# P times V of a sliding-window attention, from whole 128-key tiles to two row tiles of 64 keys, in a gated mixer kernel on one core

## The chip, the cores and the metric

The kernel runs on one NeuronCore of a Trainium2 chip. TensorE (PE, with its weight loads shown as PEld), VectorE (DVE), ScalarE (ACT), GpSimd (POOL) and the DMA queues that SyncE (SP) and ACT start work side by side and wait for one another through semaphores. The metric is the device time of one execution in microseconds (us), lower is better; a time is given as the median of several runs.

## The reference

An attention branch A (2048 tokens, 512 channels, 32 heads of 16 channels, a causal window of 256 keys), an MLP branch B (LayerNorm, 512 to 1792, GELU, back to 512), and a gate between them, all in float32:

```python
qkv = (x @ wqkv).reshape(B, S, 3, H, Dh)          # H = 32, Dh = 16, S = 2048
scores = einsum("bhqd,bhkd->bhqk", q, k) * Dh ** -0.5
mask = (idx[:, None] - idx[None, :] >= 0) & (idx[:, None] - idx[None, :] < 256)
p = softmax(where(mask, scores, -1e9))
a = einsum("bhqk,bhkd->bhqd", p, v).reshape(B, S, D) @ wo
h = gelu(layernorm(x) @ w1 + b1)                  # F = 1792
b = h @ w2 + b2
g = sigmoid((x * gate_w).sum(-1))
out = g * a + (1 - g) * b
```

A key reaches the 256 queries from its own on. So a tile of 128 keys reaches 128 + 256 = 384 queries, and a tile of 64 keys 64 + 256 = 320.

## The kernel before, in words

The work falls into three stages.

**First stage.** The projections to q, k and v (`qk_unit` line 302, `v_unit` line 334), the row statistics, and the splits of the inputs. Most products are made from float32 values split into a high and a low part (type fp32r), three matmuls for one; P times V is not split, both of its operands are plain float32. The values V stand in one tile `vs` of 16 blocks of 128 keys, with 17 columns to a head: 16 channels and a column of ones (`memset`, line 583), so that the same product also gives the row sums of P.

**Second stage.** It works off four kinds of steps, in an order that is written out by hand in the string `ORDER` (`run`, line 748):

- `S` (`s_pair`, line 353): scores of one block of 128 queries for two heads, only to find the largest score of each query: two matmuls in row tiles of 64 partitions side by side (line 362), then a masked copy and a maximum on DVE (lines 371 and 372). Every fourth block of queries its maxima go through DRAM into the operands of the next kind of step (`put_max`).
- `T` (`st_pair`, line 409): the transposed scores, 128 keys by up to 384 queries for two heads (line 418), exp on ACT (line 420) into a tile of P (eight slots, `p_tile`), and POOL sets what lies outside the window to zero (line 422). Two `T` steps fill one P tile of a block of keys kb and a group p of four heads.
- `P` (`pv`, line 429): P times V of a group p of four heads for the 256 queries with number j, or for 512 queries where two `P` stand side by side in the string and j is even. The four heads of a group are four column tiles of 32 columns. For 256 queries four blocks of keys count, one *step* each: 256, 128, 256 and 128 queries wide; for 512 queries six steps. At j = 0 the two steps before the first query fall away. A step is four matmuls, one for each head, and the trace shows each of these float32 matmuls as two weight loads and two matmuls. The product stands in the first bank of a pair of banks, is copied out on ACT (line 136, through `copy`), in the last steps on DVE (line 451), and is put beside its neighbour in one of two staging buffers (`sums`, names x in the profile), so that 512 queries are stored by one DMA of 256 KB into `osc` in DRAM (line 458, or 460 at the end).
- `f` (`fill`, line 719): one of the 24 steps of an MLP unit (`mlp1_unit`, line 639): two matmuls in row tiles of 64 partitions, 512 wide (line 651). The result goes through ACT to `hp` in DRAM.

PSUM is four pairs of banks. `S`, `T` and `P` each take the next pair of a ring (`two`, line 117; the string `PICK` says where the second in the ring is taken in place of the first); an MLP unit holds one pair for its 24 steps. A pair comes free when its reader (ACT or DVE) is done.

**Last stage.** 56 items (c, f): a chunk c of 512 tokens and a block f of 128 hidden channels. For each, `hp` is loaded (`load_h`, six items ahead), GELU runs on ACT (line 707), DVE splits it (lines 711 and 133), and PE does 12 matmuls of 512 columns (`mlp2`, line 881). The second weights come by `load_w2`, six items ahead, for the first chunk only. All of these take their buffers from one ring of 28 tiles `t`. Beside this, once for each chunk, `attn_out` (line 817) loads the row sums `su` and the products `oa` from `osc`, DVE takes the reciprocal (line 833), it goes through DRAM to `ra`, DVE multiplies (line 839), ACT and DVE split the result, and PE multiplies by wo (line 850), 12 matmuls for each of the four blocks of 128 tokens. At the end of a chunk line 889 (first chunk) or 895 takes the sum out of PSUM.

## Time and profile before

| | us |
|---|---|
| median of 3 runs (lowest, highest) | 690.24 (689.75, 690.57) |
| the profiled execution | 689.64 |
| its span, first to last instruction | 687.8 |
| first stage, until the first P times V comes near | 0 to 149 |
| second stage | 149 to 484 |
| last stage | 484 to 687.8 |

The granted TensorE clock was 0.999 of full speed over the span. What lies around the span is 1.84 us. How to read the rows that follow in the prediction: in a table of stages each engine has its busy time and, in brackets, its number of instructions; then come the granted clock, the mean busy share of the DMA engines and GB/s. A row of the time line starts with the start of a group of instructions and the time from its first start to its last end, so groups that overlap in the pipelined PE have times that overlap. A matmul's record runs on after its last column has entered, so the pace of PE is read from one start to the next and not from lengths. `128x256 f32 x8` means eight matmuls 256 columns wide with 128 partitions of contraction, `64*128 64x512` one with 64 partitions.

### The profile page before, as it was taken

The numbers are of one execution on the slowest core, as the hardware profiler recorded it, in microseconds if no ns is written. First come the engines' busy times: TensorE is split into PE (matmuls) and PEld (weight loads), VectorE is DVE, ScalarE is ACT, GpSimd is POOL, SyncE is SP. The second block draws the span as 40 slices with busy tenths as digits, with TensorE's granted clock in tenths as the row PEclk, the third lists the DMA queues.
The fourth block names the chain that finished last, engine by engine and source line by source line (L and its number), as shares of the span: only waits on it lengthen the run. The fifth ranks groups of instructions, "written<-read, shape, count | busy, mean of one in ns | idle before, by whom it ended". The sixth has DMA issues, their size and how long they took to land.

```text
span 687.8 us, 15593 instructions
## 1 busy us (share of the span) xinstructions
PE 681.1 (99%) x5674; PEld 535.5 (78%) x5674; DVE 476.4 (69%) x970; ACT 384.6 (56%) x637; POOL 265.9 (39%) x622
## 2 busy tenths in 40 slices
PE   9999999999999999999999999999999999999997
PEld 6887777877768777877787777777787888888886
DVE  6737789968777787777686877855575545556454
ACT  6438453457677776877758777687633224123231
POOL 6800156426666664765656566568000000000000
PEclk9999999999999999999999999999999999999999
DMA  8998888786575767566676555527876450841801
GB/s 322 354 290 266 278 262 267 217 253 224 176 211 173 247 211 228 174 214 188 190 240 207 168 185 153 178 96 240 288 238 204 143 173 5 275 126 41 253 1 62
DMA packets 89620, 137.91 MB, mean 200 GB/s; under 512 B 13160, under 2 KB 36648, under 8 KB 89416
## 3 DMA queue, kind: packets, MB, share of 16 engines
q1 hardware_dynamic: 81384, 128.72, 59.1%
q10 hardware_dynamic: 8160, 8.19, 3.9%
q8 instruction: 45, 0.74, 0.4%
q14 instruction: 31, 0.25, 0.1%
HBM read 81.53 MB, written 54.30 MB: 197 GB/s over the span
## 4 chain that ended last, share of the span: by engine, by line
PE 96%; ACT 1%; DVE 1%; DMA 1%; issue 0%; POOL 0%; SPq 0%; DVEq 0%; ACTq 0%
PE ps_b L651 22%; PE ps_a L881 22%; PE ps_b L441 13%; PE ps_d L308 12%; PE ps_b L418 7%; PE ps_b L362 7%; PE ps_d L338 7%; PE ps_o L850 6%; PE ps_d L295 1%; PE ps_x L362 1%; DMA qk<-qk 1%; PE ps_x L279 1%; ACT x L420 0%; DVE us L895 0%; DVE us L889 0%; ACT pb L420 0%
## 5 line engine op out<-in xcount | busy, mean ns | idle before, releaser
L651 PE MATMUL ps_b<-x,w 64*128 64x512 f32 x1344 | 207.1, 393 | 0.0
L881 PE MATMUL ps_a<-x,t 128*128 128x512 f32 x648 | 150.2, 389 | 0.2 <-DVE t L711 0.2
L372 DVE TENSOR_REDUCE mx<-ps_b 128x2 f32<-128x512 f32 x208 | 144.1, 693 | 7.1
L881 PEld LDWEIGHTS ps_a<-x,t 128*128 128x128 f32 x648 | 121.5, 188 | 26.2 <-DVE t L711 0.6
L651 PEld LDWEIGHTS ps_b<-x,w 64*128 64x128 f32 x1344 | 127.4, 186 | 10.5 <-ACT x L136 0.3
L371 DVE COPY_PREDICATED ps_b<-tri,ps_b 128x256 f32<-128x256 uint8 x208 | 88.4, 425 | 52.7 <-PE ps_b L362 40.6
L422 POOL TENSOR_SCALAR_AFFINE_SELECT pa<-pa 128x256 f32<-128x256 f32 x192 | 74.2, 414 | 57.7 <-ACT pa L420 56.7
L420 ACT ACTIVATE pa<-ps_b 128x768 f32<-128x768 f32 x96 | 76.5, 813 | 24.7 <-PE ps_b L418 13.3
L418 PE MATMUL ps_b<-qk 50*128 50x384 f32 (+5 forms) x512 | 87.8, 339 | 0.1
L308 PE MATMUL ps_d<-x,w 128*128 128x512 f32 x360 | 84.7, 390 | 0.0
L362 PE MATMUL ps_b<-qk 62*128 62x384 f32 (+3 forms) x472 | 83.0, 345 | 1.0 <-DMA qk<-qk 0.8
L308 PEld LDWEIGHTS ps_d<-x,w 128*128 128x128 f32 x360 | 67.3, 188 | 14.5 <-issue 0.5
L420 ACT ACTIVATE pb<-ps_b 128x768 f32<-128x768 f32 (+2 forms) x96 | 66.2, 706 | 20.5 <-PE ps_b L418 9.7
L422 POOL TENSOR_SCALAR_AFFINE_SELECT pb<-pb 128x256 f32<-128x256 f32 x160 | 62.2, 415 | 37.4 <-ACT pb L420 36.9
L707 ACT ACTIVATE t<-t,b1s 128x512 f32<-128x512 f32 x56 | 38.6, 716 | 44.0 <-DMA t<-hp 43.6
L418 PEld LDWEIGHTS ps_b<-qk 50*128 50x128 f32 (+1 forms) x512 | 48.8, 184 | 16.0 <-issue 3.2
L422 POOL TENSOR_SCALAR_AFFINE_SELECT x<-x 128x256 f32<-128x256 f32 x128 | 49.3, 414 | 29.7 <-ACT x L420 29.3
L420 ACT ACTIVATE x<-ps_b 128x768 f32<-128x768 f32 x64 | 50.7, 813 | 14.0 <-PE ps_b L418 9.7
L362 PEld LDWEIGHTS ps_b<-qk 62*128 62x128 f32 (+1 forms) x472 | 45.1, 184 | 17.2 <-issue 3.9
L338 PE MATMUL ps_d<-wv,x 128*128 128x512 f32 x192 | 46.7, 394 | 0.0
L850 PE MATMUL ps_o<-w,t 128*128 128x512 f32 x192 | 46.1, 389 | 0.0
L441 PE MATMUL ps_b<-pa,v 128*32 128x128 f32 (+2 forms) x704 | 42.9, 345 | 0.3 <-ACT x L420 0.2
(96 smaller groups left out, 757.1 us busy)
## 6 DMA issues: line engine op xcount, KB each, us to landing
qk<-qk SPq DMA_DIRECT2D x112, 196.0 KB
t<-hp SPq DMA_DIRECT2D x56, 256.0 KB
hp<-t SPq DMA_DIRECT2D x54, 256.0 KB
qk<-t SPq DMA_DIRECT2D x48, 256.0 KB
osc<-x SPq DMA_DIRECT2D x31, 256.0 KB
t<-in_w SPq DMA_DIRECT2D x28, 256.0 KB
w<-w SPq DMA_DIRECT2D x28, 256.0 KB
qk<-t ACTq DMA_DIRECT2D x24, 256.0 KB
```

The lines of the kernel that those rows point to most:

```text
L308: pe.matmul(o, a[:, dt * 128:(dt + 1) * 128], b[:, dt * C:(dt + 1) * C], start=n == 0, stop=n == 11)
L338: pe.matmul(o, x[:, a:a + 128], wvs[dt][:, k], start=n == 0, stop=n == 11)
L362: pe.matmul(o[:, e, :n], qs[pr][r:k, qb * 128:qb * 128 + 128], ks[pr][r:k, t0:t0 + n], start=True, stop=True)
L371: dve.copy_predicated(o[:, :, :128], tri, o[:, :, 256:384])
L372: dve.tensor_reduce(m, o[:, :, :256], mybir.AxisListType.X, ALU.max)
L418: pe.matmul(o[:, e, :w], ks[pr][r:k, kb * 128:kb * 128 + 128], qs[pr][r:k, kb * 128:kb * 128 + w], start=True, stop=True)
L420: act.activation(pt[:, :, :w], o[:, :, :w], AF.Exp, scale=0.25)
L422: pool.affine_select(out=pt[:, :, a:a + 128], in_=pt[:, :, a:a + 128], pattern=[[0, 2], [sgn, 128]], base=b, channel_multiplier=-sgn, comp ...
L441: pe.matmul(a[32 * h:32 * h + 32, at:at + w], vs[:, kb, v:v + 32], pts[p, kb][:, h, fr:fr + w], start=n == 0, stop=n == len(parts) - 1, sk ...
L651: pe.matmul(o[:, e], w[kt // 4][r:r + 64, k, m:m + 128], y[r:r + 64, a:a + C], start=n == 0, stop=n == 23)
L850: pe.matmul(a, x[:, g], wos[g][:, k], start=n == 0, stop=n == 11)
L881: pe.matmul(accs[c][b], x[:, b * 128:(b + 1) * 128], w, start=f == 0 and n == 0, stop=f == FT - 1 and n == 2)
```

## The change

P times V is now cut into two row tiles of 64 keys. The upper and the lower 64 keys of a block each take only the 320 queries that they reach, in two row tiles of the array (rows 0 to 63 and 64 to 127), with the four heads still in four column tiles: eight matmuls in a step in place of four, each with half of the contraction. The upper half of the keys adds into the first bank of the pair, the lower half into the second, and the steps are sorted so that pieces of the same or nearly the same width stand together: for 256 queries 256, 192, 128 and 64 wide. Nothing on the chip adds the two banks in this stage: both are copied (one ACT copy of 2 x 256 columns for each 256 queries) and stored as halves, one DMA of 256 KB for each 256 queries. `osc` is laid out anew and twice as large. There are still two staging buffers, but each now holds 256 queries; where a third copy comes up with two stores still unissued, the oldest store is issued first. The copy on DVE in the last steps is gone, all copies are on ACT.

In the last stage both halves are loaded (eight DMAs of 256 KB for the products of a chunk, four for the sums, two writes of the reciprocals) and DVE adds them: one add of 128x128 before the reciprocal and one of 128x512 ahead of each multiplication of line 839. To make room the ring of 28 tiles becomes rings of their own: 8 for the loads of `hp`, 6 for the split parts, 5 for the raw second weights and 4 for the rest; the second weights are loaded four items ahead in place of six.

`ORDER` and `PICK` are new. Both orders have 652 `f`, 256 `T`, 236 `S` and 63 `P` letters, and one `P` more runs after each.

The rows below show one P times V as PE has it, the same one (heads 0 to 3, queries 768 to 1023) before and now, with the steps around it; pa, pb and x are slots of P tiles, v is V, ps_b a pair of banks, qk the score operands. Before:

```order
L362 MATMUL ps_b_262_1541<-qk_79 128x384 x2
L418 MATMUL ps_b_261_1535<-qk_79 128x384 x2
L441 MATMUL ps_b_260_1529<-x_254_1522,v_80 32x256 x4
L441 MATMUL ps_b_260_1529<-pb_1524,v_80 32x128 x4
L441 MATMUL ps_b_260_1529<-pb_1524,v_80 32x256 x4
L441 MATMUL ps_b_260_1529<-pb_1524,v_80 32x128 x4
L362 MATMUL ps_b_263_1546<-qk_79 128x384 x2
```

The same place in the changed kernel, where line 418 has become 420, 362 has become 364 and 441 has become 450:

```order
L364 MATMUL ps_b_260_1530<-qk_79 128x384 x2
L450 MATMUL ps_b_261_1536<-pb_1524,v_80 32x256 x4
L450 MATMUL ps_b_261_1536<-x_254_1522,v_80 32x256 x4
L450 MATMUL ps_b_261_1536<-x_254_1522,v_80 32x192 x4
L450 MATMUL ps_b_261_1536<-pb_1524,v_80 32x192 x4
L450 MATMUL ps_b_261_1536<-pb_1524,v_80 32x128 x8
L450 MATMUL ps_b_261_1536<-pb_1524,v_80 32x64 x8
L364 MATMUL ps_b_262_1541<-qk_79 128x384 x2
```

There are 16 matmuls before and 32 now; each pair of rows (or an x8) is one step of two row tiles, and the widths of a step's row tile come to 640 in place of 768.

The next rows are ACT's at the place in the second stage where the copies of P times V stand closest together. L136 (L138 now) is the copy of a bank, with x_253 and x_254 the staging buffers where a ps_b is copied to x; the copies to t are those of an MLP unit, and L420 (L422 now) is the exp. Before:

```order
L136 ACTIVATE t_1811<-ps_b_263_1546 128x512
L136 ACTIVATE t_1814<-ps_b_263_1546 128x512
L420 ACTIVATE pb_1524<-ps_b_261_1535 128x768
L136 ACTIVATE x_253_1521<-ps_b_260_1529 128x256
L420 ACTIVATE pb_1524<-ps_b_263_1546 128x768
L420 ACTIVATE pb_1524<-ps_b_261_1535 128x768
L136 ACTIVATE x_254_1522<-ps_b_260_1529 128x256
L420 ACTIVATE pa_1523<-ps_b_261_1535 128x768
L136 ACTIVATE x_254_1522<-ps_b_260_1529 128x256
```

Now:

```order
L138 ACTIVATE t_1811<-ps_b_261_1536 128x512
L138 ACTIVATE t_1814<-ps_b_261_1536 128x512
L138 ACTIVATE x_253_1521<-ps_b_260_1530 128x512
L138 ACTIVATE x_254_1522<-ps_b_260_1530 128x512
L138 ACTIVATE x_253_1521<-ps_b_261_1536 128x512
L422 ACTIVATE pb_1524<-ps_b_262_1541 128x768
L422 ACTIVATE pb_1524<-ps_b_261_1536 128x768
```

Three copies, each twice as wide, now stand in a row, the third into the buffer that the first filled.

Last, DVE at the start of the product with wo for the second chunk, where `oa` holds the products, `ra` the reciprocals, and the rows of L711 and L133 (L714 and L135 now) split GELU's result. Before:

```order
L839 TENSOR_TENSOR oa_7177<-oa_7177,ra_7178 128x4x128
L133 TENSOR_TENSOR t_7470<-oa_7177,t_7469 128x512
L711 CAST t_7475<-t_7296 128x512
L133 TENSOR_TENSOR t_7476<-t_7296,t_7475 128x512
L839 TENSOR_TENSOR oa_7177<-oa_7177,ra_7178 128x4x128
```

Now:

```order
L850 TENSOR_TENSOR oa_8163<-oa_8163 128x4x128
L851 TENSOR_TENSOR oa_8163<-oa_8163,ra_8164 128x4x128
L135 TENSOR_TENSOR t_8467<-oa_8163,t_8466 128x512
L714 CAST hl_8472<-s_8289 128x512
L135 TENSOR_TENSOR hl_8473<-s_8289,hl_8472 128x512
L850 TENSOR_TENSOR oa_8163<-oa_8163 128x4x128
```

One add stands ahead of each multiplication, and the split parts now have the ring hl.

The diff, with the two strings cut to a line each:

```diff
-ORDER = ("STSfffffTfSfffTSfffTfSffTfSfffSfTffffSPSfTfSfffTSfffTffTfSfTfffSffSTfSffTfSfffSTPTSTPSSTPSffTSffffTS"
+ORDER = ("TSffTfSfTfSfffTSfffTfSffTfSfffTSfffTfSffffSffTfSfffTSfffTfSfTfSfffSTfSffTfSfSffSPPPTfSfTffSffTfSffTf"
...
-    def t2(dt=F32, shape=(128, 512)):
-        return get("work", "t", nt[0], shape, dt)
+    def t2(dt=F32, shape=(128, 512), tag="t"):
+        if len(nt) == 1:
+            return get("work", "t", nt[0], shape, dt)
+        return get("work", tag, nt[1][tag], shape, dt)
...
-    osc = dram.tile([8, 128, S], F32, name="osc")
+    osc = dram.tile([8, 8 * 128, 512], F32, name="osc")
...
-    def pv(p, j, last, both):
+    stores = []
+
+    def pv(p, j, both):
         flush()
-        a = two()[:, 0]
-        if both:
-            parts = ((-1, 0, 128, 256), (-2, 0, 256, 128), (0, 0, 0, 384), (1, 128, 0, 384), (2, 256, 0, 256),
-                     (3, 384, 0, 128))[0 if j else 2:]
-        else:
-            parts = ((-1, 0, 128, 256), (-2, 0, 256, 128), (0, 0, 0, 256), (1, 128, 0, 128))[0 if j else 2:]
-        for n, (d, at, fr, w) in enumerate(parts):
-            kb = 2 * j + d
-            for h in range(4):
-                v = (4 * p + h) * VW
-                pe.matmul(a[32 * h:32 * h + 32, at:at + w], vs[:, kb, v:v + 32], pts[p, kb][:, h, fr:fr + w],
-                          start=n == 0, stop=n == len(parts) - 1, skip_group_check=True, tile_position=(0, 32 * h))
-        if j % 2 == 0:
-            sums.append(sums.pop(0))
-            acc[p] = sums[-1]
-        s = acc[p]
-        o = j % 2 * 256
-        if both:
-            copy(s, a)
-        elif last:
-            dve.tensor_copy(s[:, o:o + 256], a[:, :256])
-        else:
-            copy(s[:, o:o + 256], a[:, :256])
-        if j % 2 or both:
-            j += both
-            to = osc[p, :, (j - 1) * 256:(j + 1) * 256]
+        a = two()
+        q, w = 256 * j, 512 if both else 256
+        parts = []
+        for r in range(2):
+            seen = []
+            for kb in range(max(2 * j - 2, 0), 2 * j + w // 128):
+                k = kb * 128
+                fr, to = max(q, k + 64 * r * (kb > 0)), min(q + w, k + 64 * r + 320)
+                seen.append((fr - to, kb, fr - q, to - q, fr - k, to - k))
+            parts.append(sorted(seen))
+        for n, pieces in enumerate(zip(*parts)):
+            for r, (_, kb, *at) in enumerate(pieces):
+                rows = slice(64 * r, 64 * r + 64)
+                for h in range(4):
+                    v = (4 * p + h) * VW
+                    pe.matmul(a[32 * h:32 * h + 32, r, at[0]:at[1]], vs[rows, kb, v:v + 32], pts[p, kb][rows, h, at[2]:at[3]],
+                              start=n == 0, stop=n == len(parts[0]) - 1, skip_group_check=True, tile_position=(64 * r, 32 * h))
+        for n in range(1 + both):
+            s = sums.pop(0)
+            sums.append(s)
+            if len(stores) > 1:
+                stores.pop(0)()
+            copy(s.rearrange("p (r n) -> p r n", r=2), a[:, :, 256 * n:256 * n + 256])
+            to = osc[j + n, 128 * p:128 * p + 128]
             if lt:
-                after(1, lambda: sp.dma_start(to, s))
+                stores.append(lambda to=to, s=s: sp.dma_start(to, s))
+                after(1, lambda fn=stores[-1]: fn in stores and (stores.remove(fn), fn()))
             else:
                 act.dma_start(to, s)
...
-    nt[0] = 28
+    nt.append({"t": 4, "s": 8, "hl": 6, "wr": 5})
...
-        su = small("su", 1, (128, 128))
-        for g in range(NG):
-            sp.dma_start(su[32 * g:32 * g + 32],
-                         view(osc, [32 * S, HG], [128, 4], [1, 128], off=(g * 256 + 16) * S + c * C))
+        su = get("work", "su", 1, (128, 2, 128))
+        rows = 8 * 128 * 512
+        for n in range(2):
+            for r in range(2):
+                sp.dma_start(su[64 * n:64 * n + 64, r],
+                             view(osc, [32 * 512, H], [128, 2], [1, 128], off=(2 * c + n) * rows + 16 * 512 + 256 * r))
...
-            sp.dma_start(o[:, g], view(osc, [32 * S, HG], [S, DH], [1, C], off=g * 256 * S + c * C))
+            for n in range(2):
+                sp.dma_start(oa[:, g, n].rearrange("p r n -> p (r n)"),
+                             view(osc, [32 * 512, HG], [512, DH], [1, 512], off=(2 * c + n) * rows + g * 256 * 512))
...
-            dve.reciprocal(su, su)
-            sp.dma_start(view(rd, [128, 128], [1, 128]), su)
+            dve.tensor_tensor(out=su[:, 0], in0=su[:, 0], in1=su[:, 1], op=ALU.add)
+            dve.reciprocal(su[:, 0], su[:, 0])
+            for n in range(2):
+                sp.dma_start(view(rd, [C, H], [128, 2], [1, 128], off=256 * n), su[64 * n:64 * n + 64, 0])
...
-        def scale(b, o, r):
-            dve.tensor_tensor(out=o, in0=o, in1=r, op=ALU.mult)
+        def scale(b):
+            q = b % 2 * 128
+            o, more = (oa[:, :, b // 2, e, q:q + 128] for e in range(2))
+            dve.tensor_tensor(out=o, in0=o, in1=more, op=ALU.add)
+            dve.tensor_tensor(out=o, in0=o, in1=r[:, :, b * 128:b * 128 + 128], op=ALU.mult)
...
-        for k in (n + 6,):
-            c, f = item(k)
-            if f >= 0:
-                if c == 0 and f > 5:
-                    waiting["w", f] = load_w2(f)
-                waiting[c, f] = load_h(c, f)
+        c, f = item(n + 4)
+        if c == 0 and f > 5:
+            waiting["w", f] = load_w2(f)
+        c, f = item(n + 6)
+        if f >= 0:
+            waiting[c, f] = load_h(c, f)
```

50 lines of the change are left out of this document (25 added, 25 removed).

## The prediction

> **What bounds the kernel now.** The page first: busy time by engine, and the chain of waits that ended last, by engine.
>
> ```profile
> PE 681.1 (99%) x5674; PEld 535.5 (78%) x5674; DVE 476.4 (69%) x970; ACT 384.6 (56%) x637; POOL 265.9 (39%) x622
> PE 96%; ACT 1%; DVE 1%; DMA 1%; issue 0%; POOL 0%; SPq 0%; DVEq 0%; ACTq 0%
> ```
>
> PE carries 96% of the chain. But a share over the whole span says nothing of the stage that changes, so next the busy times by stage, second and last:
>
> ```profile
> 149.00:484.00 335.00, 333.67 (x4126) 255.82 (x4124) 253.94 (x572) 246.50 (x379) 208.80 (x548) 1.00 0.62 195
> 484.00:688.00 204.00, 199.77 (x892) 164.24 (x888) 112.46 (x196) 62.87 (x99) 0.00 (x0) 1.00 0.47 151
> ```
>
> In the second stage PE is busy for all but 1.3 of 335 us at the full granted clock, ACT for 74%, DVE for 76%. A time saved on PE there is saved from the end, as long as ACT and DVE, at three quarters, keep their lead. Busy is not the same as streaming, though, so I look at two P times V and what stands between them in PE's time line:
>
> ```profile
> 165.01 0.64 PE L441 MATMUL ps_b<-pa,v 128*32 128x256 f32 x8
> 165.47 0.40 PE L441 MATMUL ps_b<-x,v 128*32 128x128 f32 x8
> 165.69 0.62 PE L441 MATMUL ps_b<-pb,v 128*32 128x256 f32 x8
> 166.12 0.40 PE L441 MATMUL ps_b<-x,v 128*32 128x128 f32 x8
> 166.45 0.61 PE L362 MATMUL ps_b<-qk 62*128 62x384 f32 x4
> 166.90 0.34 PE L418 MATMUL ps_b<-qk 64*128 64x384 f32 x2
> 167.17 0.64 PE L441 MATMUL ps_b<-x,v 128*32 128x256 f32 x8
> ```
>
> From start to start a step 256 wide takes 0.43 us (165.69 to 166.12) and one 128 wide 0.22 (165.47 to 165.69): 1.69 ns a column, in proportion to width, with no fixed part to speak of. The four heads run side by side, since eight matmuls take this time together.
>
> **The change part by part.** *Columns.* The two strings and the window give the steps. Before: 112 steps of 256, 112 of 128 and 8 of 384 columns, 46,080 in all; the trace has 1856 matmuls on line 441, which is 232 steps of four heads with two matmuls each:
>
> ```profile
> 149.00:484.00 335.00, 89.91 (x1856) 52.88 (x1856) 1.00 0.62 195
> ```
>
> Their time is 112 x 0.43 + 112 x 0.22 + 8 x 0.65 = 78.0 us (384 columns as 256 and 128). Now, by the wider of the two pieces: 61 steps of 256, 61 of 128, 53 of 192, 53 of 64, 4 of 320 and 2 of 384, 39,040 columns. At 1.69 ns that is 66.0 us, a gain of 12.0, if eight tiles run side by side as four do, and if a pass of the narrow steps is not held up by the issue of 16 weight loads and matmuls in place of 8. The trace of before shows no eight tiles at once, so both need bounds. For the rows: MLP steps in two row tiles, and a product with wo over the whole array, both 512 wide:
>
> ```profile
> 480.67 1.60 PE L651 MATMUL ps_b<-x,w 64*128 64x512 f32 x12
> 534.34 2.72 PE ps_o L850 x12
> ```
>
> Twelve matmuls over the whole array take 2.72 us, 0.23 each; twelve in two row tiles end within 1.60. Two row tiles do run together and into two banks. For the issue: the first weight loads of a P times V, and how long one lasts:
>
> ```profile
> 153.35 0.16 PEld L441 LDWEIGHTS ps_b<-pa,v 128*32 128x32 f32 x8 [0.31 <-issue]
> L441 PEld LDWEIGHTS ps_b<-pa,v x704: 105/110/110, 153.4 to 478.8; 128*32 128x32 f32 x176
> ```
>
> Eight loads of 0.11 us end within 0.16, so they start 7 ns apart, with matmuls in between. At 7 ns eight tiles are started in 0.056 us; a pass (half a step) of 64 columns streams in 0.054. So only the narrowest steps come up to the issue, and 12.0 stays. The slow end, that today's 128-wide step is itself paced by the issue (8 loads and matmuls in 0.22, 27.5 ns a pair), is a rival below. I take 12.0, since the 7 ns is of the same instructions.
>
> The Trainium skill, page "TensorE: Matmul & The Clock Gate", section "Wait — 56ns, not 53.3ns?", has matmuls never start closer than about 25 ns however narrow they are. That speaks against this change: eight tiles would need 0.2 us a pass, and as an estimate from that page the sum would be 709 us. The 7 ns above says otherwise for matmuls of different tiles, though only in bursts.
>
> *Entering and leaving.* From a score matmul of 384 columns (0.17 us at the 0.23 for 512) to the P times V behind it pass 0.27 us (166.90 to 167.17), 0.10 too much; from the last step 128 wide to the next score 0.33, 0.11 too much, and the two score pairs behind it take 0.45 in place of 0.34, 0.11 more. So about 0.3 us for each group of neighbouring P. The old order has 55 groups, the new one 52: a gain of 0.9. That the array still has to empty is shown where 128-row matmuls meet the scores in the first stage:
>
> ```profile
> 65.68 2.88 PE L308 MATMUL ps_d<-x,w 128*128 128x512 f32 x12
> 68.49 0.61 PE L362 MATMUL ps_x<-qk 62*128 62x384 f32 x4
> 69.03 2.35 PE L308 MATMUL ps_d<-x,w 128*128 128x512 f32 x9
> ```
>
> There two pairs of 0.17 take 0.54 from start to start, 0.2 too much, though no column tiles are in play. The Trainium skill, page "TensorEngine Tiling (Array Packing)", section "Key Properties", says that changing the tiling mode drains the engine; by that rule nothing changes here, as 64x32 is another mode than 64x128, and these rows agree with it.
>
> *Copies.* ACT's rows and the one of DVE that goes:
>
> ```profile
> L136 ACT ACTIVATE x<-ps_b 128x256 f32<-128x256 f32 x50 | 19.3, 385 | 21.7 <-PE ps_b L441 21.1 <-ACT pb L420 0.3
> L136 ACT ACTIVATE x<-ps_b 128x512 f32<-128x512 f32 x4 | 2.4, 600 | 4.0 <-issue 4.0
> L451 DVE COPY x<-ps_b 128x256 f32<-128x256 f32 x6 | 2.6, 426 | 12.1 <-PE ps_b L441 7.0 <-DMA hp<-t 5.1
> PEld ps_b L441 <- ACT x L136: 5.6, 23, 0.3
> ```
>
> Before: 19.3 + 2.4 = 21.7 us on ACT and 2.6 on DVE. Now 64 copies of 512 columns at 0.60: 38.4 us, all on ACT, 16.7 more. ACT then has 263 us in a stage of about 324, 81%: still beside PE, not on its path. But PE already waits for such copies, 23 times for 5.6 us in all, because each frees a pair of banks, and each copy is 0.215 longer. At worst all 52 groups pay that: 11.2 us. At best nothing, because a single P times V is 0.21 shorter on PE (128 columns less), so that its pair is held as long as before. I take 1.0: near the low end by that balance, but with ACT fuller.
>
> The two staging buffers now turn over every second copy. At two places (heads 0 to 3 and 4 to 7, the start of each) three copies stand in a row, and the third waits for the store of the first; behind it on ACT are exps, for which POOL and the next P times V wait. The trace gives a store's issue but not its landing:
>
> ```profile
> L458 SPq DMA_DIRECT2D osc<-x x31: 319/343/1092, 164.8 to 479.5; - x31
> 523.59 0.95 DVE L833 RECIPROCAL su<-su 128x128 f32<-128x128 f32 x1 [6.20 <-DMA su<-osc]
> ```
>
> Between 0.34 (an issue) and 6.2 (the longest wait for a DMA on `osc`) each; ACT has other exps done by then and the ring three other pairs, so I take 0.25 of PE's time each, 0.5. The 32 more stores of 256 KB (8.4 MB) raise the DMA share of this stage from 0.62 to about 0.72, and the score operands come by the same queue; PE waited for these once:
>
> ```profile
> L362 PE MATMUL ps_b<-qk 62*128 62x384 f32 x208 | 72.4, 354 | 1.0 <-DMA qk<-qk 0.8
> ```
>
> That is 0.8 us for one of eight groups of heads, so 0 to 6 now; I take 0, as the rest were early enough to leave no wait.
>
> *Last stage.* The added work on DVE, priced by the multiplication and the reciprocal of the same sizes, and the one place where PE waited:
>
> ```profile
> L839 DVE TENSOR_TENSOR oa<-oa,ra 128x512 f32<-128x512 f32 x16 | 11.0, 685 | 8.9 <-DMA ra<-rd 8.9
> L833 DVE RECIPROCAL su<-su 128x128 f32<-128x128 f32 x4 | 3.8, 949 | 10.6 <-DMA su<-osc 10.6
> 528.33 6.01 PE L881 MATMUL ps_a<-x,t 128*128 128x512 f32 x24 [0.16 <-DVE t L711]
> ```
>
> Sixteen adds of 0.685 are 11.0 us, four of at most 0.95 another 3.8. DVE goes from 112.5 to about 127 of 204 us, and the adds stand in items whose PE work is 24 matmuls (5.4 us) while DVE has some 4.6, so they are hidden. At the end of the first chunk there is no cover: DVE came 6.2 us late through the sums, and PE waited 0.16. The longer add could make this 1 to 2 us; the loads in rings of their own no longer wait for PE to free a shared tile, so the sums may come earlier and the wait go. I take 0. The rings cost nothing while six split tiles (three items) cover DVE's lead; the raw second weights still have three items, over 8 us.
>
> *The sum.* 689.64 - 12.0 - 0.9 + 1.0 + 0.5 = 678.2 for the profiled execution. The median is 0.60 above it, so 678.8.
>
> **The rivals.** *ACT takes it back.* If every group waits for a longer copy (11.2 in place of 1.0), 689.0; the halfway case is 684. For it: 74% becomes 81%, with every copy in one engine's order. Against it: the hold of a pair is unchanged and the new order may place around it.
>
> *The issue paces the steps (slower).* If 27.5 ns for each weight load and matmul is a limit, a step of 16 pairs cannot take less than 0.44 us, and the 228 steps up to 256 wide cost 100.3, with the wider ones 103.8: 25.8 more, 716.6 us. Against it: the 7 ns bursts, and steps in exact proportion to width. For it: nothing in the trace issues faster for longer than a few dozen instructions. It decides from about 17 ns a pair: there the 114 steps of 64 and 128 columns take 0.27 each, and the gain is gone.
>
> *The row tiles take turns (slower).* The upper and lower halves have 38,912 and 38,400 columns; one after the other, 130.7 us, 742.9. Against it: the MLP rows. For it: these have no column tiles.
>
> *No emptying.* If row tiles of 64 among themselves cost no change, 52 x 0.3 = 15.6 more are saved, 663. Against it: the first-stage rows.
>
> **How the numbers follow.** My forecast has 0.72 (677 to 682), ACT taking some of it back 0.14, the issue 0.05, turns 0.03, no emptying 0.06. The likeliest gives 678.8. The range is 675.5 to 686: below it lies only the case without emptying, above it the two slower cases and the worse half of ACT's, 0.2 in all. It takes in the unknown costs up to about 7 us together. A measurement of this kernel can tell 0.2%, 1.4 us, from no change. Faster: 0.72 + 0.06 + 0.12 of ACT's 0.14 = 0.90; the same 0.02; slower 0.08.
>
> **What would show it.** In the new time line, steps of 64, 128, 192 and 256 columns should take about 0.11, 0.22, 0.32 and 0.43 from start to start with 16 matmuls each; a 64-wide one at 0.2 or more speaks for the issue. The second stage should shrink by 10 to 13 us, the last stage stay within 1 us of 204. Waits of PE for ACT's copies should stay below about 8 us in all; if they double, ACT takes it back. The forecast is wrong if the time lies above 686, or if it is reached by a shorter last stage.

## The result, and the profile after

| | us |
|---|---|
| before, median of 4 runs beside it (lowest, highest) | 690.40 (689.75, 692.02) |
| after, median of 4 runs (lowest, highest) | 718.40 (714.17, 722.37) |
| ratio, 95% interval | 1.040 (1.033 to 1.047) |
| the profiled execution of after, its span | 722.37, 720.7 |

The forecast was 678.8, within 675.5 to 686.0. The change makes the kernel slower by 28 us. Four disturbed executions (two of the products alone in the new order, one of the old order, one of the adds put back) are left out of the times and ratios below.

First the page of after: busy time by engine, and the chain of waits that ended last.

```profile
PE 688.0 (95%) x7562; PEld 551.8 (77%) x7562; DVE 485.2 (67%) x984; ACT 396.5 (55%) x647; POOL 266.8 (37%) x622
PE 71%; DMA 17%; ACT 3%; DVE 3%; issue 3%; SPq 2%; ACTq 0%; POOL 0%; DVEq 0%
```

Before, PE had 96% of the chain and DMA 1%. Now a sixth of it is transfers. Where, the stages tell: busy time by stage, the second stage and the last, in the order PE, PEld, DVE, ACT, POOL.

```profile
149.00:515.00 366.00, 347.27 (x6083) 280.83 (x6079) 257.98 (x580) 263.14 (x395) 210.21 (x551) 0.98 0.67 214
515.00:721.00 206.00, 194.98 (x840) 157.87 (x840) 121.69 (x206) 59.29 (x95) 0.00 (x0) 0.99 0.49 152
```

The stages do not end at these round times. The groups of the MLP matmuls give the true borders: first and last start stand behind the durations, for line 654 (second stage) and for the first group of line 893 (last stage); the two rows of before come first.

```profile
L651 PE MATMUL ps_b<-x,w x1344: 383/392/497, 145.8 to 486.7; 64*128 64x512 f32 x192
L881 PE MATMUL ps_a<-x,x x24: 389/389/500, 487.1 to 492.4; 128*128 128x512 f32 x24
```

```profile
L654 PE MATMUL ps_b<-x,w x1344: 383/392/732, 147.6 to 507.5; 64*128 64x512 f32 x192
L893 PE MATMUL ps_a<-x,x x24: 387/389/497, 507.8 to 513.2; 128*128 128x512 f32 x24
```

The second stage went from 341.3 us (145.8 to 487.1) to 360.2 (147.6 to 507.8), the last from 200.7 to the end of the span to 212.9. So 19 us are lost in the second stage and 12 in the last, in an execution 4 us above the median; the other 1.8 lie in the first stage, whose code did not change and which ended between 145.7 and 149.4 in the profiles shown from here on, whatever the kernel.

What PE and ACT wait for, out of the list of waits (total, times, longest):

```profile
ACT x L138 <- DMA osc<-x: 12.9, 5, 4.6
PEld ps_b L420 <- ACT x L138: 9.5, 14, 4.7
PEld ps_b L364 <- ACT x L138: 6.2, 9, 3.2
PE ps_b L420 <- ACT x L138: 5.9, 3, 4.3
PE ps_a L893 <- DVE hl L714: 5.4, 3, 2.5
```

The first row is new: the copy of P times V waits for a store of the staging buffer to land. The next rows show the score steps waiting for that copy, since it holds their pair of banks. Before, PE's one stop of note in this stage was 0.8 us, for the score operands. The time line at the place with three copies in a row shows how it comes about:

```profile
166.96 1.08 ACT L138 ACTIVATE x<-ps_b 128x512 f32<-128x512 f32 x2 [1.09 <-PE ps_b L450]
167.58 0.34 SPq L460 DMA_DIRECT2D osc<-x  x1
172.68 0.60 ACT L138 ACTIVATE x<-ps_b 128x512 f32<-128x512 f32 x1 [4.64 <-DMA osc<-x]
173.33 0.69 PE L420 MATMUL ps_b<-qk 64*128 64x384 f32 x2 [4.33 <-ACT x L138]
```

The store issued at 167.58 lands 5.0 us later; until then ACT stands still with its exponentials queued behind the copy, and PE follows it for 4.33 us. Then comes a second price, seen in the stages of 2 us right there (the column before the DMA share is the granted clock):

```profile
170.00:172.00 2.00, 0.00 (x0) 0.00 (x0) 0.04 (x1) 0.00 (x0) 0.00 (x0) 1.00 1.03 381
172.00:174.00 2.00, 0.67 (x4) 0.67 (x6) 0.00 (x0) 1.30 (x2) 0.00 (x0) 0.52 0.28 102
174.00:176.00 2.00, 2.00 (x14) 1.63 (x12) 0.66 (x2) 0.81 (x1) 1.54 (x4) 0.50 0.37 138
176.00:178.00 2.00, 2.00 (x14) 1.72 (x12) 1.20 (x3) 0.81 (x1) 0.67 (x2) 0.50 0.79 227
```

At the end of the stop the clock goes to half, and it stays there until 178.9, a little past these rows. What PE does from 173.33 on takes twice as long, some 2.8 us lost behind a stop of 4.33. The Trainium skill, page "TensorE: Matmul & The Clock Gate", section "Part 1: The HAM clock gate (the "warmup" mystery)", has the clock fall to half after an idle window of about 3.4 us and come back after a busy one; this stop of 4.33 us agrees.

The last stage loses its time where a chunk's sums and products are loaded. Pieces of the chain of waits there, start and length:

```profile
530.71 8.47 DMA oa<-osc
539.20 7.61 DMA s<-hp
546.83 4.90 DMA su<-osc
```

And the time line where the last of these ends:

```profile
543.67 3.67 SPq L825 DMA_DIRECT2D su<-osc  x4
551.95 0.29 DVE L840 TENSOR_TENSOR su<-su 128x128 f32<-128x128 f32 x1 [3.57 <-DMA su<-osc]
553.56 2.02 PE L893 MATMUL ps_a<-x,hl 128*128 128x512 f32 x4 [2.54 <-DVE hl L714]
```

The add of the sums waits for the loads, the split of GELU's result stands behind it on DVE, and PE waits 2.54 us for that split. Over the whole last stage PE waits 5.4 us in three for such splits (the last row of the list of waits) and 2.7 in two for the split of the products:

```profile
PE ps_o L862 <- ACT t L138: 2.7, 2, 1.7
```

Before, its waits in this stage came to 0.2 us.

### The profile page after: what moved, and what is told of

Its sections match the earlier page's. It is cut to its first block, busy times and chain, and to the rows that moved or that the text cites. A ratio compares the mean times of both kernels' runs of the same rounds, so it can differ in the third digit from the quotient of the medians.

```text
span 720.7 us, 19538 instructions
## 1 busy us (share of the span) xinstructions
PE 688.0 (95%) x7562; PEld 551.8 (77%) x7562; DVE 485.2 (67%) x984; ACT 396.5 (55%) x647; POOL 266.8 (37%) x622
## 4 chain that ended last, share of the span: by engine, by line
PE 71%; DMA 17%; ACT 3%; DVE 3%; issue 3%; SPq 2%; ACTq 0%; POOL 0%; DVEq 0%
PE ps_b L654 20%; PE ps_d L310 10%; PE ps_b L450 9%; PE ps_a L893 8%; PE ps_o L862 6%; PE ps_b L420 6%; PE ps_b L364 6%; PE ps_d L340 5%; DMA osc<-x 3%; DMA s<-hp 3%; DMA ra<-rd 3%; DMA oa<-osc 2%; ACT x L138 1%; DMA b2s<-in_b 1%; DMA qk<-qk 1%
## 5 line engine op out<-in xcount | busy, mean ns | idle before, releaser
L654 PE MATMUL ps_b<-x,w 64*128 64x512 f32 x1344 | 215.7, 401 | 0.1
L893 PE MATMUL ps_a<-x,hl 128*128 128x512 f32 x648 | 153.5, 394 | 5.5 <-DVE hl L714 5.4
L893 PEld LDWEIGHTS ps_a<-x,hl 128*128 128x128 f32 x648 | 122.1, 190 | 34.4 <-DVE hl L714 4.7
L420 PE MATMUL ps_b<-qk 50*128 50x384 f32 (+5 forms) x512 | 91.0, 348 | 8.8 <-ACT x L138 5.9
L364 PE MATMUL ps_b<-qk 62*128 62x384 f32 (+2 forms) x472 | 84.8, 353 | 4.5 <-ACT x L138 3.8
L422 ACT ACTIVATE pa<-ps_b 128x768 f32<-128x768 f32 x96 | 76.4, 813 | 20.0 <-PE ps_b L420 10.9
L422 ACT ACTIVATE pb<-ps_b 128x768 f32<-128x768 f32 (+2 forms) x96 | 66.4, 708 | 18.4 <-PE ps_b L420 11.4
L420 PEld LDWEIGHTS ps_b<-qk 64*128 64x128 f32 (+1 forms) x512 | 49.8, 187 | 28.4 <-ACT x L138 9.5
L364 PEld LDWEIGHTS ps_b<-qk 62*128 62x128 f32 x472 | 45.5, 187 | 21.2 <-ACT x L138 6.2
L138 ACT ACTIVATE x<-ps_b 128x512 f32<-128x512 f32 x64 | 38.0, 599 | 42.5 <-DMA osc<-x 12.9
L710 ACT ACTIVATE s<-s,b1s 128x512 f32<-128x512 f32 x54 | 36.8, 713 | 38.5 <-DMA s<-hp 38.1
L422 ACT ACTIVATE x<-ps_b 128x768 f32<-128x768 f32 x64 | 50.6, 813 | 8.0 <-PE ps_b L420 5.1
L450 PE MATMUL ps_b<-pa,v 64*32 64x192 f32 (+4 forms) x1472 | 53.0, 308 | 1.7 <-issue 1.2
L450 PE MATMUL ps_b<-pb,v 64*32 64x256 f32 (+4 forms) x1264 | 47.9, 301 | 1.7 <-ACT x L138 1.2
```

The costliest lines, as they stand in the source:

```text
L138: act.activation(dst, src, AF.Copy)
L364: pe.matmul(o[:, e, :n], qs[pr][r:k, qb * 128:qb * 128 + 128], ks[pr][r:k, t0:t0 + n], start=True, stop=True)
L420: pe.matmul(o[:, e, :w], ks[pr][r:k, kb * 128:kb * 128 + 128], qs[pr][r:k, kb * 128:kb * 128 + w], start=True, stop=True)
L422: act.activation(pt[:, :, :w], o[:, :, :w], AF.Exp, scale=0.25)
L450: pe.matmul(a[32 * h:32 * h + 32, r, at[0]:at[1]], vs[rows, kb, v:v + 32], pts[p, kb][rows, h, at[2]:at[3]], start=n == 0, stop=n == len(p ...
L654: pe.matmul(o[:, e], w[kt // 4][r:r + 64, k, m:m + 128], y[r:r + 64, a:a + C], start=n == 0, stop=n == 23)
```

## The experiments

The theory to be tested: the row-tiled products gain little; the second half of the results, copied, stored and loaded again, costs the rest, in three separate places (ACT's copies, the staging buffers, the last stage). The rivals: the issue of 16 pairs of weight load and matmul a step is the whole cause; the new order is; ACT's fullness is all of it; VectorE's adds are.

**The products alone, old order.** `pv` of after in the kernel before, with only the first bank copied:

```diff
-        a = two()[:, 0]
...
+        a = two()
...
+        a = a[:, 0]
         if j % 2 == 0:
             sums.append(sums.pop(0))
```

> The kernel before with only its P times V matmuls changed: row tiles of 64 keys in two banks, but only the first bank is copied (the 256 or 512 queries of the upper keys), stored once per 512 queries as before; the order of steps and the last stage are those of before. It leaves out the lower keys' half of the sums. Theory (staging buffers that wait for their stores, the clock that halves behind the idle stretches, and more transfers in the last stage make the change slow; the matmuls themselves gain some 7 us): 681 to 686 us, no idle stretch of TensorE above 1.5 us in the second stage. Rival, the issue of 16 short matmuls a step is what makes it slow: above 700 us. Rival, the new order is the cause: also 678 to 686, so this run does not tell it from the theory.

Measured: 692.7 us beside 689.5, ratio 1.0042 (1.0021 to 1.0064) over ten runs. Issue as the whole cause falls: that rival had it above 700. But the theory's gain is not there either. The trace shows three stops of PE of 1.4 us and more, the longest inside a P times V:

```profile
181.43 0.56 PE L446 MATMUL ps_b<-pa,v 64*32 64x128 f32 x29
183.76 0.30 PE L446 MATMUL ps_b<-pa,v 64*32 64x64 f32 x3 [1.77 <-issue]
```

Twenty-nine of 32 matmuls are out, and the last three come 1.77 us late; the trace shows no data that they wait for. On the queue that loads instructions (59 loads of 16 KB here, 45 before) one had started some 0.8 us before PE ran dry; at each of the three stops PE went on 2.3 to 2.6 us after the start of such a load.

**The products alone, new order.** The same with the two strings of after.

> As the run with the products alone (row tiles, only the first bank copied and stored, the last stage of before; it leaves out the lower keys' half of the sums), but with the new order of steps and the new choice of banks. Theory: the matmuls gain some 6 us, and in the old order the gain was eaten by stops of TensorE for its own instructions where two P times V steps follow each other (1.5 to 2 us each, three of them); the new order parts most of these: 680 to 686 us. Rival, the new order is no better for this: 690 to 694 us.

Measured: 689.8 us (eight runs) beside 690.0, ratio 0.9999 (0.9976 to 1.0022). No gain and no loss: the theory's time was missed, and the time lies at the lower edge of the rival's. The new order with the products of before was not run, so this is what products and order bring together. The same kernel once more, for its profile:

> The row-tiled products alone in the new order once more, for its profile (the lower keys' half of the sums is left out). Its time was that of the kernel before. Theory: a P times V step gains only some 0.15 us, since its last passes of 64 columns are paced by issue and not by columns, and the waits ahead of these steps grow by about as much as the steps gain: steps of 78 to 80 us from their first matmul to the next other one against 86.2, entries longer by 3 to 5 us, no idle stretch over 1.5 us. Rival: the gain is there in full (74 us) and other stops of 10 us eat it.

Measured: 688.4 us, one run, beside 689.9. Busy time of the P times V matmuls (and of their weight loads), in before and here:

```profile
147.00:515.00 368.00, 89.91 (x1856) 52.88 (x1856) 1.00 0.64 202
```

```profile
147.00:515.00 368.00, 81.32 (x3744) 67.45 (x3744) 1.00 0.65 206
```

They gain 8.6 us, and yet the second stage is only 2.7 shorter, by the first and last starts of the MLP matmuls:

```profile
L657 PE MATMUL ps_b<-x,w x1344: 383/392/499, 147.9 to 486.2; 64*128 64x512 f32 x192
L887 PE MATMUL ps_a<-x,x x24: 387/389/497, 486.5 to 491.9; 128*128 128x512 f32 x24
```

That is 338.6 in place of 341.3. Where the rest went can be counted from the starts of the matmuls in the two traces, since the times from one start to the next add up to the stage. From its first matmul to the next other one, a group of P times V takes 86.2 us in all before and 79.1 here, 7.1 less. The score steps take 100.5 in place of 96.3: 2.8 of these 4.2 us stand between a score step and the P times V behind it, 2.3 between an S and the T behind it, and other places give a little back.

The 7.1 is less than the 12.0 of columns, and the steps' tail shows one reason. The best view of it is one P times V of after, from its 128-wide matmuls to the next score:

```profile
187.28 0.32 PE L450 MATMUL ps_b<-pb,v 64*32 64x128 f32 x8
...
187.46 0.27 PE L450 MATMUL ps_b<-pa,v 64*32 64x64 f32 x4
187.66 0.44 PE L364 MATMUL ps_b<-qk 62*128 62x384 f32 x2
```

A 64-wide matmul's record lasts 0.215 us at the least; the four in one row last 0.27, so they start about 18 ns apart, and not 7. As for the 4.2 us, the waits ahead of P times V and of T are for other things now ("issue" means that the trace shows nothing that the engine waited for):

```profile
PEld ps_b L446 <- issue: 7.8, 25, 1.5
PEld ps_b L418 <- DVE mx L372: 6.7, 32, 0.4
PEld ps_b L446 <- POOL pa L422: 3.2, 10, 0.7
PEld ps_b L446 <- POOL pb L422: 3.2, 10, 0.4
PEld ps_b L446 <- POOL x L422: 2.9, 8, 0.7
```

Before these were 3.8 for issue (17 times), 1.7 for DVE's maxima (8 times), and 0.2, 0.9 and 0.8 for POOL's masks. In return the waits for ACT's copies, 7.0 us in 30, fell to 0.4. Weight loads idle a little in any case, and all waits of the weight loads together did not grow, so these totals are no loss of PE's. They fit the longer times ahead of P times V (POOL's masks, issue) and of T (DVE's maxima), but no run takes the three apart. Of the expectation, the steps (79.1 us), the longer entries (2.8, a little under the 3 to 5) and the missing long stops (one of 1.3 us) were right.

**The second copy alone.** As the last kernel, with ACT copying the second bank into the place that the first bank's copy then takes:

```diff
-            copy(s[:, o:o + 256], a[:, :256])
+            copy(s[:, o:o + 256], a[:, 1, :256])
+            copy(s[:, o:o + 256], a[:, 0, :256])
```

> The row-tiled products in the new order with before's stores and last stage, and ScalarE copies the second bank too, into the place that the copy of the first bank then overwrites (so the lower keys' half is left out of the result, and ScalarE has some 20 us more to do, as in the changed kernel, but nothing more is stored or loaded). Theory: what the third buffer and the smaller loads don't give back, some 10 us, is ScalarE's longer copies, behind which exponentials start late: 696 to 702 us. Rival, ScalarE has the room and the rest of the loss is the stores themselves: 689 to 692 us.

Measured: 699.1 us beside 689.9, ratio 1.0131 (1.0091 to 1.0172), 9 us more than the products alone, with not a byte more to move. The rival (ACT has room) falls. The rows that came in:

```profile
PEld ps_b L418 <- ACT x L136: 5.9, 18, 0.6
PEld ps_b L362 <- ACT x L136: 4.5, 13, 0.6
PE ps_b L446 <- ACT x L136: 2.4, 7, 0.5
```

In the kernel without the second copy the first two of these were 0.2 each, once, and the third was absent. ACT's busy time in the second stage:

```profile
147.00:494.00 347.00, 338.38 (x6061) 272.77 (x6057) 260.08 (x585) 264.62 (x434) 208.85 (x551) 1.00 0.60 192
```

264.6 of 347 us, 76%: a quarter of ACT is idle, and the copies still reach PE, since T, S and P steps wait for the pairs of banks that a copy holds. One thing differs from the changed kernel: for 256 queries two copies of 0.38 us follow one another here, and one of 0.60 there, so a pair is held longer and the 9 us are rather too much for the changed kernel.

**A third staging buffer**, in after, with the stores put out early only at three pending and the ring t cut from 6 to 5 for the room:

```diff
-            if len(stores) > 1:
+            if len(stores) > 2:
...
-    nt[0] = 6
+    nt[0] = 5
...
+    sums.append(get("work", "st", 1, (128, 512)))
```

> The changed kernel with a third staging buffer for the copies of P times V, a store put out early only when more than two are pending, and the ring of tiles t in the second stage cut from 6 to 5 to make room. Theory: the waits of the copy for a store's landing (12.9 us in 5 waits on ScalarE, 14 to 17 us on TensorE behind them) and most of the 17 us at half clock go: 698 to 708 us. Rival, issue pace: 716 to 720. Rival, the last stage alone: 716 to 720. Rival, ScalarE too full: 716 to 720, as its work is the same.

Measured: 712.3 us, ratio 1.034 (1.029 to 1.039); after had 1.040. The interval overlaps that of after, so the size of the step is read from another pair of runs, further down. The wait itself is gone:

```profile
ACT x L138 <- DMA osc<-x: 0.7, 1, 0.7
```

0.7 us once, in place of 12.9 in five, and the clock stays whole where it was 0.93 and 0.97:

```profile
150.00:200.00 50.00, 47.89 (x790) 38.39 (x790) 39.68 (x90) 35.14 (x52) 28.02 (x78) 1.00 0.68 222
200.00:250.00 50.00, 48.50 (x873) 37.79 (x870) 37.12 (x89) 39.42 (x60) 32.43 (x84) 1.00 0.74 235
```

The time lies above the theory's 698 to 708: the last stage is still that of after, and by the run above ACT's longer copies are late next.

**The last stage with one half.** After, with product loads of 256 columns in place of 512, half the loads of the sums, and no adds:

```diff
-                sp.dma_start(oa[:, g, n].rearrange("p r n -> p (r n)"),
-                             view(osc, [32 * 512, HG], [512, DH], [1, 512], off=...))
+                sp.dma_start(oa[:, g, n, 0],
+                             view(osc, [32 * 512, HG], [512, DH], [1, 256], off=...))
...
-            dve.tensor_tensor(out=o, in0=o, in1=more, op=ALU.add)
```

> The changed kernel with the last stage reading only the first half (256 of 512 columns of each stored row, so 128 KB loads of oa and half the loads of su) and without the adds; it leaves out the lower keys' half of the sums. The second stage is that of the changed kernel. Theory: the last stage gets back most of its 12 us, the second stage none: 706 to 712 us. Rival, issue pace or staging buffers alone: 716 to 720.

Measured: 706.9 us, ratio 1.0252 (1.0221 to 1.0283), as the theory has it, 11.5 below after. From the first matmul of line 891 at 501.6 to the end of the span at 704.5 the last stage takes 202.9 us, against 212.9 in after and 200.7 in before, and PE's waits in it are down to 0.5 us:

```profile
L891 PE MATMUL ps_a<-x,x x24: 388/389/500, 501.6 to 506.9; 128*128 128x512 f32 x24
PE ps_a L891 <- DVE hl L714: 0.5, 1, 0.5
```

The new rings and the shorter lead of the second weights are still in this kernel, so they are not what costs the 10 us. **The same with the adds put back**, each adding a half to itself:

> The run that loads one half in the last stage, with the adds put back (each adds the upper keys' half to itself, so the lower keys' half is left out of the result). Theory, the doubled transfers of the stored sums cost the last stage its 11 us: 704 to 709 us, as without the adds. Rival, the adds on VectorE cost it: 714 to 720 us.

Measured: 706.1 us, ratio 1.0235 (1.019 to 1.0281): the adds cost nothing that can be measured, the loads do. The number of product loads is that of after, so it is their size, or the two more loads of the sums, and not the product loads' issue.

**Both mended**: the third buffer and the last stage with one half, in one kernel.

> The changed kernel with a third staging buffer (ring of tiles t 5 instead of 6) and with the last stage loading only the upper keys' half, without the adds (the lower keys' half is left out of the result). Theory, store waits and last stage are separate costs that add: 718.4 less 6 less 11.5: 699 to 703 us. Rival, they are one cost (both are the same pressure on the transfers): 705 to 708 us. Rival, together they are all of the loss: 686 to 692 us.

Measured: 701.5 us, ratio 1.0156 (1.0124 to 1.0188). Against the half loads without the third buffer (1.0252) that is 6.6 us less, against the third buffer without the half loads (1.034) 12.7 less, both clear of their intervals. The costs are separate and add, within what the intervals allow. The stages of the profiles, from their borders as above, say the same place by place (one execution each):

| kernel | second stage, us | last stage, us |
|---|---|---|
| before | 341.3 | 200.7 |
| products alone, new order | 338.6 | 200.1 |
| with the second copy | 348.2 | 200.0 |
| both mended | 348.9 | 201.5 |
| one half loaded | 354.4 | 202.9 |
| third buffer | 349.4 | 212.5 |
| after | 360.2 | 212.9 |

**The old order** with all else of the change:

> The changed kernel with the old order of steps and the old choice of banks. Theory: the copies of P times V still share two staging buffers and each step with both halves of 512 queries still needs both, so some store waits stay and some go: 708 to 722 us. Rival, the new order is the cause of the loss: 684 to 692 us. Rival, issue pace: 716 to 722.

Measured: 737.1 us, ratio 1.0664 (1.0612 to 1.0716). The order as the cause falls, and the theory's range is missed on the high side: the new order is worth 19 us to the changed kernel. The old one ran into the staging buffers still more often:

```profile
ACT x L138 <- DMA osc<-x: 22.1, 9, 3.7
```

**The halves added early**: the products in the new order, ACT copies the first bank, DVE adds the second into the staging buffer one step later, stores and last stage as before.

```diff
+        copy(to, a[:, 0, :w])
+
+        def add():
+            dve.tensor_tensor(out=to, in0=to, in1=a[:, 1, :w], op=ALU.add)
+
+        late.append(add)
```

> Row tiles in the new order, but the halves are added in the second stage: ScalarE copies the first bank as before, VectorE adds the second bank into the staging buffer one step later, and one store per 512 queries and the last stage are those of before. It computes all that the reference does. Theory: no store wait, no doubled transfers, VectorE gets 25 to 30 us more work at 75% busy; 680 to 688 us. Rival, the issue of the short matmuls is what makes the change slow: above 700 us. Rival, VectorE's adds hold up the score reductions: 690 to 700 us.

Measured: 703.5 us, ratio 1.0196 (1.0171 to 1.0221): 15 us faster than after with the whole result, 13 slower than before. The theory's 680 to 688 was wrong. By its number the time falls to the rival "issue, above 700", but the products alone, with the same matmuls, took 690. The other rival, DVE holding up the scores, is what the waits show, worse than priced:

```profile
PEld ps_b L418 <- DVE mx L372: 8.4, 32, 0.8
PEld ps_b L418 <- DVE x L460: 6.0, 17, 0.6
```

**Narrow pieces first**, in after:

```diff
-            parts.append(sorted(seen))
+            parts.append(sorted(seen)[::-1])
```

> The changed kernel with the pieces of each P times V step taken from the narrowest to the widest, so that the short matmuls come while TensorE's queue is still full. Theory: each step's last passes are paced by the issue (some 17 ns for a load and a matmul); 52 steps by 0.1 to 0.2 us come back, less what the newest block's mask, needed earlier, costs: 710 to 716 us. Rival, the order of the pieces does nothing: 716 to 720 us. Rival, the earlier need of the newest block costs more than it brings: 720 to 730 us.

Measured: 711.4 us, ratio 1.0317 (1.0275 to 1.0358), within the theory's range, though the interval still touches that of after. And the reason given for it does not hold: the P times V matmuls are as long as in the other order, 82.2 us busy against 81.5 in after.

```profile
147.00:515.00 368.00, 82.22 (x3744) 54.87 (x3744) 0.99 0.68 221
```

The weight loads' busy time fell from 67.8 to 54.9, and PE did not gain by it. Waits for stores are shorter here (5.2 us in three); why, is not taken apart, and the gain stays without a shown cause.

**Twice the instructions, no row tiles**: the kernel before with each P times V matmul split into two of half the columns.

```diff
+            w //= 2
+            for i in (0, w):
...
-                    pe.matmul(a[32 * h:32 * h + 32, at:at + w], ...
+                    pe.matmul(a[32 * h:32 * h + 32, at + i:at + i + w], ...
```

> The kernel before with every P times V matmul split into two of half the columns: the same columns and result, 3,712 matmuls and as many weight loads where there were 1,856, and no row tiles. The 64 column passes of four tiles need 107 ns, more than 4 issues of 17 ns. Theory: the count of instructions alone costs stops for TensorE's instruction blocks of 1.5 to 2 us where two steps follow each other, three to five times, and little besides: 692 to 698 us. Rival, the count is free and the cost of the row tiles lies in the row tiles: 689 to 691 us. Rival, each issue costs 17 ns on the path: 1,856 of them 31 us, above 715 us.

Measured: 693.1 us, ratio 1.0054 (1.0032 to 1.0075). The time is in the theory's range, its mechanism is not: the trace has one stop above 0.6 us in the second stage, of 0.8, and not three to five. The matmuls take 1.1 us more than before (91.0 against 89.9):

```profile
147.00:515.00 368.00, 91.00 (x3712) 81.27 (x3712) 1.00 0.64 203
```

So 1,856 more instructions made the kernel some 3 us slower, but in this one profile the second stage is only 0.5 us longer than before; where the rest goes is not shown.

## Why the prediction was wrong, point by point

The sum had five terms. The runs put a size to each; a ratio is turned into us at 690.

| term | predicted | measured | by |
|---|---|---|---|
| columns, entering and leaving | -12.9 | 0.0 (-1.7 to +1.5) | products alone, new order |
| ACT's copies | +1.0 | +9.1, rather too much | second copy against products alone |
| third copy waits for a store | +0.5 | +6.6 (+4 by the other pair) | both mended against half loads |
| more stores, all else | 0 | +1.7, rather too little | both mended against second copy |
| last stage | 0 | +10.3 (+12.7 by the other pair) | half loads against after |

They add up to the measured 27.7 us by construction, since each run is compared with the next; what the runs show is the size of each step. The second and fourth rows are safe only as a sum, 10.8 (both mended against products alone), because of the longer hold in the run with the second copy. In both mended, with the changed kernel's own copies, weight loads waited 5.2 us in 22 for copies of P times V, against 10.9 in 32 there. And PE has two stops in it, of 1.6 and 2.2 us, that the second copy alone does not have; in the longer one, at 484.4, a copy of an MLP unit waits for a store of `hp`.

*Columns.* The step that failed is "only the narrowest steps come up to the issue, and 12.0 stays". The pace of 7 ns was read at the head of a P times V; at its tail matmuls start 18 ns apart. The prediction's own condition named it: from about 17 ns a pair the gain of the narrow steps goes. Of the 12.0 the groups kept 7.1 from start to start (8.6 by their busy time). Another 4.2 went to longer times around the score steps, where PE now waits for issue, POOL's masks and DVE's maxima; their shares are open. So the 0.9 for entering and leaving came out as a loss too: fewer groups, but each entry longer. The gain was counted from PE's share of the stage, 333.7 of 335 us, with no price for what PE would meet next. The page's floor of 25 ns (the Trainium skill, "TensorE: Matmul & The Clock Gate", section "Wait — 56ns, not 53.3ns?"), by which the prediction had 709 us, does not hold for column and row tiles: 18 ns at the tail, 7 at the head; and the products alone took 690 us. As a warning against narrow matmuls it pointed the right way.

*Copies.* "I take 1.0: near the low end by that balance" failed. The balance said that a P times V holds its pair of banks no longer, since its matmuls shrink by what the copy grows. But a later step can only wait for a pair after the matmuls have ended, so the copy's side of the balance counts and the matmuls' side does not; and the copy also delays every exponential behind it on ACT. Both show in the run with the second copy: weight loads wait 10.9 us in 32 for copies, where it was 0.4 in 2 without them, and 5.0 us in 16 for exponentials, where it was 2.8 in 11. How much each of the two costs, no run tells. The measured 9.1, even if rather too much, lies toward the bound of 11.2 and not toward 0. ACT's 81%, taken as room, was 72 to 76% in the runs, and PE waited all the same. This is the rival "ACT takes it back", with the right mechanism and 0.14 of chance; its sign came true: the weight loads' waits for copies are 15.9 us in after and were 7.0 before, though some of them lie behind the waits for stores.

*Staging buffers.* The mechanism and the place were right, the price was not: 0.25 us of PE's time at each of two places, against one stop of 4.33 us at the first alone. The upper bound of 6.2 stood in the text; the cover named ("ACT has other exps done by then") ends after one step, since later exponentials stand behind the waiting copy. The prediction also missed the other places, five waits in all, and the half clock behind a long stop.

*Last stage.* "I take 0" failed. The adds are hidden, as predicted. The loads are not: they were priced at nothing because DVE had time, but the sums come late, and through DVE's order the split of the next item comes late too. The text had this wait as "possible 1 to 2 us". PE's waits in the stage came to 8.1 us in after, 0.5 with the half loads and 0.2 before, and the step is 10 to 13 us over four chunks.

*The rivals.* Issue as the whole cause is refuted (products alone 690 to 693). Row tiles that take turns are refuted (81 us busy and not 131; the 742.9 given for them leaves out the 0.6 us of the other terms). The 663 us of a change without emptying are 27 us below what the products alone take.

## What to carry to other kernels

When the engine that bounds a stage does less, price the next engine as well: here the 7 to 9 us that PE's products gained shrank to a gain too small to measure. An engine that is a quarter idle is not free for work that holds a shared buffer or stands in order ahead of what the bound engine needs. Splitting a sum into halves that are added later means that every copy, store, buffer and load of it doubles; those cost 28 us here.

## What the runs showed of the hardware

A stop of TensorE of under 2 us can be followed by half the clock. In the products alone, old order, PE stood still for 1.77 us from 182.0 on, and shortly after it had gone on the granted clock was half:

```profile
182.00:184.00 2.00, 0.24 (x5) 0.15 (x4) 0.69 (x1) 0.00 (x0) 0.49 (x2) 1.00 0.48 152
184.00:186.00 2.00, 2.00 (x15) 1.78 (x16) 0.42 (x1) 1.85 (x3) 0.60 (x2) 0.69 0.35 129
186.00:188.00 2.00, 2.00 (x14) 1.63 (x14) 0.83 (x3) 0.72 (x2) 1.66 (x6) 0.50 0.44 136
```

The Trainium skill, page "TensorE: Matmul & The Clock Gate", section "Part 1: The HAM clock gate (the "warmup" mystery)", has an idle window of about 3.4 us for this, and here less was enough. In the same run the stops of 1.48 and 1.45 us left the clock whole.

TensorE also stopped, with no data to wait for in the trace, where two P times V of 64 matmuls followed each other within 2.5 us, in or shortly behind the second: for 1.45, 1.48 and 1.77 us in the old order, once for 1.3 in the new. Each time it went on 2.2 to 2.6 us after the start of a load of 16 KB on the queue that loads instructions, so it seems to have waited for its own instructions. In the kernel with as many matmuls that were only split there was one such stop, of 0.8 us, so the count alone does not make the long ones. What else it takes stays open.
